# Two feed-forward layers behind a memory attention: operand sums on VectorE, one room for k and v, one weight set converted at another place

## The chip, the cores and the metric

One core of a Trainium2 chip. The metric is the device time of one execution in microseconds (us), for which three runs are given; the profile is of one further execution. The engines are TensorE (PE, with its weight loads PEld), VectorE (DVE), ScalarE (ACT), GpSimd (POOL) and SyncE (SP), which issues every transfer (DMA). Each engine works through its own list of instructions in order.

## The reference

Eight batches of eight heads, 576 positions, head size 64 and 32 memories. The result of the attention, [4608, 512], goes through two feed-forward layers, 512 to 2048 to 512.

```python
a = exp(phi - max(phi, axis=2)); a = a / (sum(a, axis=2) + 1e-9)
k_m = einsum('bhsm,bhsd->bhmd', a, k)
v_m = einsum('bhsm,bhsd->bhmd', a, v)
scores = scale * (q @ k_m.T)
x = softmax(scores) @ v_m                 # then [4608, 512]
for w_in, w_out in ((moe_w_in, moe_w_out), (moe2_w_in, moe2_w_out)):
    h = x @ w_in                          # 512 x 2048, float64
    g = h * sigmoid(1.702 * h)            # second layer: sigmoid(h)
    x = g @ w_out                         # 2048 x 512, float64
```

## The kernel before

A product of float32 matrices is taken in three passes (`PASSES`): each operand is split into a high half in the type fp32r and a low half, the rest; high x high, high x low and low x high are added in PSUM. The high half is a copy on ACT, the low half a subtraction (`sub`, line 64), so nearly all subtractions of the kernel are recorded at L64 and the additions at L61. Three of the four big products use a scheme of seven products of half size in place of eight, in the order `ORDER` = 1, 2, 6, 5, 7, 3, 4; it needs sums of quarters of both operands. The weights come as 64-bit numbers; `wconv0` and `wconv1` turn them into float32 by two ACT operations, two of VectorE (L101, L102) and an addition on POOL (L104).

The program has four stages, told apart by PE's line.

Stage 1 (L332, 42 to 421 us): attention, and the first product of layer 1. It has 256 slots, 32 for each batch, of six matmuls; from slot 24 on the order on every engine is the order in which the code is written. `at(slot, when, fn)` plans a function at a slot; `emit` calls, in each slot, those of "e", then the slot's matmuls, then those of "p", "l" and "d". `plan_attention(b)` sets the steps of batch b against z = 32b - 32: load of phi, of k and v (`load_kv`), maximum over the positions (`fold_step`), exponential, the matmuls of k and v (`kv_mm`, L207), softmax, and so on. k and v come in four parts of four heads and three chunks each, with two rooms. The gated result g (L337, L338) goes from four rooms to memory (L342). The second weight matrix of layer 1 comes in four sets of four raw loads (`wo_load`, L76); sets 0 to 2 are converted during stage 1 and their sums and lows made, set 3 around the end of the stage.

Stage 2 (L514, 421 to 849): second product of layer 1. Its 168 steps are six blocks of seven products times four parts p; `seq` lists them. A step's operand is made two steps ahead by `make`: `a_prep` takes a room, ACT copies the high half (L498, tile `op`), VectorE subtracts the low half (L64). The quarters of the gated result, a11, a12, a21, a22, are loaded as `r` or `rr` (`r_fetch`). Their sums are made in place: a21 + a22 and a21 - a11 in `a_prep` behind products 1 and 2, and a22 - a11 and a12 - a11 in `a_sum` ahead of products 7 and 3:

```python
        if then:
            a_sum(*then, early)
        sub(nc.vector, t[:, :, 1], s, rd(t[:, :, 0]))
        if b >= early and i == 1:
            add(nc.gpsimd, a21, a21, a22)
        if b >= early and i == 2:
            sub(nc.gpsimd, a11, a21, a11)
```

After the four parts of a product `evac2` adds the bank to the output tile (L529). During the stage 16 raw weights of layer 2 are converted, one every seven steps. In the last block the first two weight sets of layer 2 (`w_sums`, `w_high`, `w_low`) and the operand x of stage 3 (`x_comb`, `x_high`, `x_low`) are made.

Stage 3 (L602, 849 to 1229): first product of layer 2, 48 groups of seven products. Stage 4 (L674, 1233 to 1594): second product of layer 2, with operands made three steps ahead by the same `make`.

## Time and profile before

| | |
|---|---|
| three runs | 1601.50, 1603.86, 1605.55 us (median 1603.86) |
| the profiled execution | 1600.37 us, its span 1598.6 us |
| PE busy | 1454.8 us, 91% of the span |
| DVE, ACT, POOL busy | 1214.5, 797.3, 633.0 us |
| transfers | 264.50 MB, 165 GB/s on the mean |

Busy time is the sum over an engine's instructions; that of PE also counts matmuls at a lower clock, which take longer. A group of instructions (line, engine, operation, tiles out<-in) has its count, busy time, the mean of one in ns, the idle time of the engine just before its members and what ended that. The windows give, for a stretch, the busy time of each engine with the count of its instructions, the granted share of PE's clock, the busy share of the DMA engines, and GB/s. Several instructions with one row in a timeline have their total.

### The profile page before, as it was taken

To read this page: it belongs to the slowest core of one execution; us is meant where nothing else is said; L and a number is where in the kernel's file an instruction comes from. 1 tells how busy PE (TensorE), PEld (TensorE's weight loads), DVE (VectorE), ACT (ScalarE), POOL (GpSimd) and SP (SyncE) were. 2 spreads that over 40 slices of the span, in tenths; PEclk is the share of its full clock that TensorE was granted. 3 is DMA by queue.
4 is the path that set the end of the run, shared out by engine and by line. 5 is a ranking of instruction groups with operands and counts; after the bars stand their busy time and mean duration, and the time that the engine had idled before them with its cause. 6 is when DMAs were issued, how large, how long until landed. Compare 5 with 4: busy or idle time off the path is not lost. (4 is left out here: it accounts for less than half of the span.)

```text
span 1598.6 us, 27727 instructions
## 1 busy us (share of the span) xinstructions
PE 1454.8 (91%) x10432; PEld 1354.1 (85%) x10432; DVE 1214.5 (76%) x1529; ACT 797.3 (50%) x1415; POOL 633.0 (40%) x360
## 2 busy tenths in 40 slices
PE   4788888899799999999889899999997999999998
PEld 2566777778688899888788899999997999999998
DVE  6766666577578887988897777778688877887875
ACT  4545556566534444454445556555565444444443
POOL 2423536342475454754752333333232141242250
PEclk7799999899799999999999999999998999999999
DMA  8686687764806356264433454655456245145240
GB/s 242 178 226 211 197 228 234 208 192 152 296 21 223 113 194 204 91 229 127 140 102 115 144 180 165 203 174 172 170 180 233 95 153 188 65 144 188 67 142 30
DMA packets 214470, 264.50 MB, mean 165 GB/s; under 512 B 51520, under 2 KB 185664, under 8 KB 214336
## 3 DMA queue, kind: packets, MB, share of 16 engines
q1 hardware_dynamic: 214336, 262.73, 50.8%
q8 instruction: 82, 1.34, 0.4%
q14 instruction: 52, 0.43, 0.1%
HBM read 159.91 MB, written 102.76 MB: 164 GB/s over the span
## 5 line engine op out<-in xcount | busy, mean ns | idle before, releaser
L514 PE MATMUL p<-op,wq 128*128 128x384 f32 x2016 | 381.4, 347 | 47.0 <-DVE op L64 39.9
L514 PEld LDWEIGHTS p<-op,wq 128*128 128x128 f32 x2016 | 359.9, 194 | 68.4 <-DVE op L64 58.2
L674 PE MATMUL p<-wq,op 128*128 128x256 f32 x3024 | 360.6, 282 | 4.8 <-DVE gq L616 4.8
L674 PEld LDWEIGHTS p<-wq,op 128*128 128x128 f32 x3024 | 360.4, 191 | 5.1 <-DVE gq L616 5.1
L64 DVE TENSOR_TENSOR op<-rr,op 128x768 fp32r<-128x768 f32 x216 | 298.1, 1398 | 66.8 <-ACT op L498 64.4
L498 ACT CAST op<-rr 128x768 fp32r<-128x768 f32 x216 | 178.3, 834 | 195.0 <-PE p L674 81.8
L332 PE MATMUL h<-attnT,slab 128*128 128x288 f32 x1536 | 247.3, 313 | 10.5 <-DVE g L338 9.5
L332 PEld LDWEIGHTS h<-attnT,slab 128*128 128x128 f32 x1536 | 219.0, 198 | 40.8 <-DVE g L338 21.0
L602 PE MATMUL xb<-xq,wq 128*128 128x384 f32 x1152 | 221.5, 340 | 18.3 <-POOL xq L64 7.1
L64 DVE TENSOR_TENSOR op<-r,op 128x768 fp32r<-128x768 f32 x120 | 176.0, 1478 | 73.4 <-ACT op L498 72.4
L602 PEld LDWEIGHTS xb<-xq,wq 128*128 128x128 f32 x1152 | 201.4, 189 | 26.9 <-ACT e L634 9.5
L338 DVE SCALAR_TENSOR_TENSOR g<-g,h 128x288 f32<-128x288 f32 x256 | 110.8, 445 | 103.4 <-ACT g L337 101.5
L602 PE MATMUL y<-xq,wq 128*128 128x384 f32 x864 | 166.5, 337 | 0.9 <-ACT e L662 0.7
L616 DVE SCALAR_TENSOR_TENSOR gq<-gq,e 128x384 f32<-128x384 f32 x144 | 135.9, 957 | 36.9 <-ACT gq L611 34.3
L337 ACT ACTIVATE g<-h 128x288 f32<-128x288 f32 x256 | 103.2, 414 | 113.3 <-PE h L332 76.8
L498 ACT CAST op<-r 128x768 fp32r<-128x768 f32 x120 | 99.5, 833 | 118.4 <-PE p L674 49.1
L602 PEld LDWEIGHTS y<-xq,wq 128*128 128x128 f32 x864 | 151.7, 188 | 1.7 <-ACT e L662 1.0
L64 POOL TENSOR_TENSOR wq<-wst,wq 128x512 fp32r<-128x512 f32 x59 | 86.0, 1463 | 129.7 <-ACT wq L426 109.9
L61 POOL TENSOR_TENSOR rr<-rr,r 128x768 f32<-128x768 f32 x22 | 52.9, 2430 | 213.3 <-DMA r<-gs 172.9
L611 ACT ACTIVATE gq<-e 128x384 f32<-128x384 f32 x144 | 75.2, 525 | 115.1 <-DVE e L61 112.2
L104 POOL TENSOR_TENSOR wst<-wst 128x512 int32<-128x512 int32 x24 | 34.1, 1423 | 195.0 <-DVE wst L102 113.3
L426 ACT CAST wq<-wst 128x512 fp32r<-128x512 f32 x83 | 51.2, 618 | 47.5 <-DVE wst L64 28.1
(119 smaller groups left out, 1584.1 us busy)
## 6 DMA issues: line engine op xcount, KB each, us to landing
rr<-gs SPq DMA_DIRECT2D x120, 384.0 KB, 6.2
gs<-g SPq DMA_DIRECT2D x128, 288.0 KB, 4.0
gs<-gq SPq DMA_DIRECT2D x192, 192.0 KB, 2.0
r<-gs SPq DMA_DIRECT2D x72, 384.0 KB, 5.4
xs<-o SPq DMA_DIRECT2D x24, 384.0 KB, 4.2
xr<-xs SPq DMA_DIRECT2D x24, 384.0 KB, 4.6
out_dram<-o SPq DMA_DIRECT2D x24, 384.0 KB, 3.6
q<-in_q_dram SPq DMA_DIRECT2D x124, 72.0 KB, 4.2
```

The costliest lines, as they stand in the source:

```text
L61: eng.tensor_tensor(out=out, in0=a, in1=b, op=ALU.add)
L64: eng.tensor_tensor(out=out, in0=a, in1=b, op=ALU.subtract)
L332: nc.tensor.matmul(out=h, lhsT=slab[b, f // 4, g][:, wi, f0:f0 + 128], rhs=x[:, g, xi], start=(g == 0 and n == 0), stop=(g == 1 and n == 2))
L337: nc.scalar.activation(out=t, in_=h, func=ACTF.Tanh, scale=0.851)
L338: nc.vector.scalar_tensor_tensor(out=t, in0=t, scalar=1.0, in1=h, op0=ALU.add, op1=ALU.mult)
L426: nc.scalar.copy(out=t[:, :, 0], in_=wst[m, c, k])
L498: nc.scalar.copy(out=t[:, :, 0], in_=s)
L514: nc.tensor.matmul(out=out[:, d, :HB], lhsT=w[:, s, wi, d * 128:(d + 1) * 128], rhs=t[:, s, gi], start=(start and p == 0 and s == 0 and n ...
L602: nc.tensor.matmul(out=out, lhsT=w[:, s, wi, f0:f0 + 128], rhs=x[:, s, xi], start=(start and s == 0 and n == 0), stop=(s == 1 and n == 2), ...
L611: nc.scalar.activation(out=t, in_=h, func=ACTF.Tanh)
L616: nc.vector.scalar_tensor_tensor(out=t, in0=t, scalar=1.0, in1=h, op0=ALU.add, op1=ALU.mult)
L674: nc.tensor.matmul(out=out[:, d], lhsT=t[:, u, gi, d * 128:(d + 1) * 128], rhs=w[:, u, wi], start=(start and d != 1 and p == 0 and u == 0 ...
```

## The change

All operand sums and low halves that POOL made in stages 2 to 4 go to VectorE; POOL keeps the addition of the weight conversion (L104), the lows of weight sets 0 to 2 in stage 1, and parts of the softmax. k and v get one room for four heads and all six chunks; of batches 0 and 1 the second four heads go to rooms that the weights take later. The maximum over the positions is taken in five operations of one chunk in place of three of different sizes, and the steps of the attention stand some slots earlier. g gets a fifth room. Set 3 of the weights is converted early in the last batch, into rooms of `attnT`, and moved by two transfers from SBUF to SBUF (`wo_move`) into the tile where it is used. The first eight operands of stage 2 stand in another order. The line numbers of the changed kernel differ by up to ten: L332 there is the store of g, L328 its gating on VectorE, L127 the load of k and v, L532 the addition out of PSUM.

```diff
-    def load_kv(b, g, c0):
-        t = att.tile([P, 2, 4, 3, D], F32, tag="kv", name="kv", bufs=2)
+    def load_kv(b, g):
+        t = att.tile([P, 2, 4, C6, D], F32, tag="kv", name="kv")
         for i, src in enumerate((k, v)):
...
+    def load_kv_early(b, rooms):
+        t = st["kv", b, 1] = [wo_p.tile([P, 2, C6, D], F32, tag=f"wo{n}", name="kve") for n in rooms]
...
+    def fold(b, name, op, eng):
+        x = st["phi", b]
+        t = st[name, b] = att.tile([P, H, M], F32, tag=name, name=name)
+        for c in range(1, C6):
+            eng.tensor_tensor(out=t, in0=t if c > 1 else x[:, :, 0], in1=x[:, :, c], op=op)
...
-            gt[b, f] = moe.tile([128, 2, HS], F32, tag="g", name="g", bufs=4)
+            gt[b, f] = moe.tile([128, 2, HS], F32, tag="g", name="g", bufs=5)
...
     def wo_conv0(c, k):
-        if k == 0:
+        if c == 3 and k % 2 == 0:
+            st["wos", c, k // 2] = moe.tile([128, 2, 2, 256], F32, tag="attnT", name="wos", bufs=4)
+        elif c < 3 and k == 0:
...
+    def wo_move():
+        t = stage()
+        for i in range(2):
+            nc.sync.dma_start(out=t[:, 2 * i:2 * i + 2], in_=st.pop(("wos", 3, i)))
+        wst[2, 3] = [t[:, n] for n in range(5)]
...
-    def a_sum(b, i, p, m):
+    def a_sum(b, i, p):
         if i == 7:
-            sub(nc.vector if m else nc.gpsimd, ra[b, 2, p], ra[b, 3, p], ra[b, 0, p])
+            sub(nc.vector, ra[b, 2, p], ra[b, 3, p], ra[b, 0, p])
...
-        if b >= early and i == 1:
-            add(nc.gpsimd, a21, a21, a22)
-        if b >= early and i == 2:
-            sub(nc.gpsimd, a11, a21, a11)
+        if b and i == 1:
+            add(nc.vector, a21, a21, a22)
+        if b and i == 2:
+            sub(nc.vector, a11, a21, a11)
 
     seq = [(b, i, p) for b in range(NBK) for i in ORDER for p in range(4)]
+    seq[:8] = [(0, i, p) for i in (1, 2) for p in range(3)] + [(0, 1, 3), (0, 2, 3)]
...
-        fold, mt, mr, mb, sb, ex, mm, es, norm, kt, ke = (
-            ((-4, -3, -3), -1, 0, 1, (2, 3), (3, 4), (4, 5, 6, 7), 5, 8, 10, 11) if first else
-            ((-21, -20, -20), -18, -16, -13, (-11, -9), (-9, -7), (-7, -6, -2, -1), -6, 0, 3, 4))
-        load(-24 if b == 2 else -27, load_phi, b)
+        pm, mt, mr, mb, sb, ex, mm, es, norm, kt, ke = (
+            (-4, -1, 0, 1, (2, 3), (3, 4), (4, 7), 5, 8, 10, 11) if first else
+            (-17, -14, -12, -10, (-9, -8), (-8, -7), (-6, 1), -7, 2, 4, 5) if b == 2 else
+            (-27, -24, -22, -19, (-17, -15), (-15, -13), (-11, -2), -12, 0, 3, 4))
+        load({2: -24, 3: -31}.get(b, -34), load_phi, b)
...
+        load({2: -28, 3: -31}.get(b, -34), load_kv, b, 0)
+        if first:
+            load(-34, load_kv_early, b, (11, 12, 13, 14))
+        else:
+            load(mm[0], load_kv, b, 1)
...
-    w_set(2, 148, (170, 173, z + 21, z + 22, z + 23, z + 24, z + 25),
...
+    w_convert(3, (z - 1, z - 1, z + 4, z + 6), (z + 3, z + 5, z + 8, z + 10))
+    for n in range(2, 6):
+        w_step(2, n, z + 18 + n, nc.vector, 1, 2)
...
-        at(z + 20 + n, "d", r_fetch, 0, 0, qq, p)
-    for n in range(4):
-        at(z + (18, 18, 27, 28)[n], "d", wo_load, 3, n)
-        at(z + (27, 28, 30, 31)[n], "e", wo_conv0, 3, n)
-        at(z + (27, 28, 30, 31)[n], "l", wo_conv1, 3, n)
+        at(z + 19 + n, "d", r_fetch, 0, 0, qq, p)
+    at(z + 29, "d", wo_move)
...
-    at(z + 28, "e", make, 0, ROOMS[0], 0)
-    at(z + 30, "e", make, 0, ROOMS[0], 1)
+    at(z + 26, "e", make, 0, ROOMS[0], 0)
+    at(z + 29, "e", make, 0, ROOMS[0], 1)
...
-    for n, x in enumerate((0, 1, 5, 9, 13, 17, 20)):
-        at(x, "e", w_make, 2, 3, n, nc.gpsimd, nc.vector)
+    for n, x in enumerate((3, 4, 8, 11, 14, 17, 20)):
+        at(x, "e", w_make, 2, 3, n, nc.vector, nc.vector)
...
-            at(LAST + s + 3 + n, "l", w_low, 0, c, n, nc.gpsimd)
+            at(LAST + s + 3 + n, "l", w_low, 0, c, n, nc.vector)
...
-        at(LAST + x, "l", x_low, 0, i, nc.gpsimd if i in (6, 7, 4) else nc.vector)
+        at(LAST + x, "l", x_low, 0, i, nc.vector)
...
-            at1(n + 3 + j, 3, x_comb, b, j, nc.gpsimd)
+            at1(n + 3 + j, 3, x_comb, b, j, nc.vector)
```

VectorE at the boundary of two blocks of stage 2 (`op` are low halves, `r` and `rr` loaded quarters), before:

```order
L64 TENSOR_TENSOR op_5783<-r_5629,op_5783 128x2x384
L64 TENSOR_TENSOR op_5799<-r_5647,op_5799 128x2x384
L64 TENSOR_TENSOR op_5818<-rr_5692,op_5818 128x2x384
L64 TENSOR_TENSOR op_5837<-rr_5692,op_5837 128x2x384
L64 TENSOR_TENSOR op_5853<-rr_5649,op_5853 128x2x384
L64 TENSOR_TENSOR op_5869<-rr_5649,op_5869 128x2x384
L64 TENSOR_TENSOR op_5890<-rr_5695,op_5890 128x2x384
L101 TENSOR_SCALAR stg_5887<-stg_5887 128x512
```

and in the changed kernel:

```order
L64 TENSOR_TENSOR op_5765<-r_5611,op_5765 128x2x384
L61 TENSOR_TENSOR r_5530<-r_5530,rr_5710 128x768
L64 TENSOR_TENSOR op_5781<-r_5629,op_5781 128x2x384
L61 TENSOR_TENSOR r_5551<-r_5551,rr_5710 128x768
L64 TENSOR_TENSOR op_5800<-rr_5674,op_5800 128x2x384
L61 TENSOR_TENSOR r_5572<-r_5572,rr_5747 128x768
L64 TENSOR_TENSOR op_5819<-rr_5674,op_5819 128x2x384
L61 TENSOR_TENSOR r_5593<-r_5593,rr_5747 128x768
L64 TENSOR_TENSOR op_5835<-rr_5631,op_5835 128x2x384
L64 TENSOR_TENSOR r_5611<-r_5530,r_5611 128x768
L64 TENSOR_TENSOR op_5851<-rr_5631,op_5851 128x2x384
L64 TENSOR_TENSOR r_5629<-r_5551,r_5629 128x768
```

Six sums, which stood in POOL's list at the same place, stand now between the low halves; the four at L61 read a quarter of the next block that has just been loaded (`rr_5710`, `rr_5747`).

VectorE around the first steps of stage 2 (`g` is the gated result, `wst` the stage tile of weight set 3, `wq` a weight half), before:

```order
L64 TENSOR_TENSOR op_5251<-r_5113,op_5251 128x2x384
L338 SCALAR_TENSOR_TENSOR g_5262<-g_5262,h_5255 128x288
L101 TENSOR_SCALAR wst_5194<-wst_5194 128x2x256
L102 SCALAR_TENSOR_TENSOR wst_5194<-raw_5211,wst_5194 128x2x256
L338 SCALAR_TENSOR_TENSOR g_5262<-g_5262,h_5273 128x288
L101 TENSOR_SCALAR wst_5194<-wst_5194 128x2x256
L102 SCALAR_TENSOR_TENSOR wst_5194<-raw_5235,wst_5194 128x2x256
L64 TENSOR_TENSOR wst_5194<-wst_5194 128x512 x2
L64 TENSOR_TENSOR op_5305<-rr_5126,op_5305 128x2x384
```

and in the changed kernel:

```order
L64 TENSOR_TENSOR op_5280<-rr_5121,op_5280 128x2x384
L64 TENSOR_TENSOR op_5296<-rr_5138,op_5296 128x2x384
L64 TENSOR_TENSOR op_5311<-rr_5138,op_5311 128x2x384
L61 TENSOR_TENSOR r_5172<-r_5172,rr_5184 128x768
L64 TENSOR_TENSOR wst_5242<-wst_5242 128x512 x2
L64 TENSOR_TENSOR wq_5329<-wst_5242,wq_5329 128x2x256
L64 TENSOR_TENSOR op_5332<-rr_5153,op_5332 128x2x384
```

The conversion of set 3 (L101, L102) has left this place, low halves stand next to each other, and the sums of the set stand behind the third of them.

SP in the second batch of stage 1, around the loads of k and v of a later batch and of w_out (`raw`), before:

```order
L128 DMA kv_1646<-in_k_dram 96x4x192
L128 DMA kv_1646<-in_v_dram 96x4x192
L76 DMA raw_1649<-in_moe_w_out_dram 128x1024
L342 DMA gs0_5_90<-g_1588 128x576
L128 DMA kv_1695<-in_k_dram 96x4x192
L128 DMA kv_1695<-in_v_dram 96x4x192
```

and in the changed kernel, with all four heads in one load for k and one for v:

```order
L76 DMA raw_1567<-in_moe_w_out_dram 128x1024
L76 DMA raw_1569<-in_moe_w_out_dram 128x1024
L127 DMA kv_1606<-in_k_dram 96x4x384
L127 DMA kv_1606<-in_v_dram 96x4x384
L332 DMA gs0_4_89<-g_1532 128x576
L332 DMA gs0_5_90<-g_1564 128x576
L76 DMA raw_1663<-in_moe_w_out_dram 128x1024
```

Before, the third raw load stood between the two halves of k and v; now k and v stand ahead of it.

## Rows read from the trace of the kernel before

**Rows 1.** The page, section 1: busy us and share of the span by engine.
```profile
PE 1454.8 (91%) x10432; PEld 1354.1 (85%) x10432; DVE 1214.5 (76%) x1529; ACT 797.3 (50%) x1415; POOL 633.0 (40%) x360
```

**Rows 2.** Windows: stages 2, 1, 4; length, busy by engine, clock, DMA share, GB/s.
```profile
421.10:849.30 428.20, 381.20 (x2018) 359.80 (x2017) 355.78 (x277) 190.82 (x258) 247.00 (x117) 0.96 0.44 148
42.40:421.10 378.70, 330.70 (x3203) 272.29 (x3202) 254.86 (x538) 211.08 (x488) 143.13 (x115) 0.93 0.70 207
...
1233.50:1594.10 360.60, 360.57 (x3024) 360.36 (x3024) 276.89 (x245) 153.69 (x189) 103.34 (x42) 0.99 0.36 124
```

**Rows 3.** Windows: a stretch of stage 3 in which PE never waits; columns as above.
```profile
1000.00:1040.00 40.00, 40.00 (x231) 40.00 (x230) 30.96 (x43) 23.05 (x47) 14.44 (x9) 1.00 0.61 205
```

**Rows 4.** Windows of L514 alone: blocks 0, 4 and 5; length, PE, PEld, clock, DMA, GB/s.
```profile
421.10:505.40 84.30, 68.72 (x337) 63.96 (x338) 0.87 0.46 157
...
703.50:768.90 65.40, 61.46 (x338) 58.00 (x337) 1.00 0.49 170
768.90:849.30 80.40, 65.72 (x337) 62.08 (x335) 0.94 0.26 80
```

**Rows 5.** Waits of PE, 421 to 850: us, times, longest.
```profile
PE p L514 <- DVE op L64: 39.9, 45, 5.1
```

**Rows 6.** Groups of DVE by shape, 1248 to 1290: busy, mean ns, idle before.
```profile
L64 DVE TENSOR_TENSOR op<-rr,op 128x768 fp32r<-128x768 f32 x15 | 14.1, 953 | 2.7 <-ACT op L498 2.7
```

**Rows 7.** The same of DVE, 1290.8 to 1310.
```profile
L64 DVE TENSOR_TENSOR op<-rr,op 128x768 fp32r<-128x768 f32 x6 | 13.2, 2234 | 2.0 <-ACT op L498 1.9
```

**Rows 8.** The same of POOL, 1290.8 to 1310.
```profile
L61 POOL TENSOR_TENSOR rr<-rr,r 128x768 f32<-128x768 f32 x4 | 9.6, 2428 | 43.5 <-DMA r<-gs 43.5
```

**Rows 9.** The same of DVE, then of POOL, 421 to 850 (stage 2).
```profile
L64 DVE TENSOR_TENSOR op<-rr,op 128x768 fp32r<-128x768 f32 x96 | 142.6, 1510 | 25.2 <-ACT op L498 23.3 <-DMA rr<-gs 1.1
...
L104 POOL TENSOR_TENSOR stg<-stg,wst 128x512 int32<-128x512 int32 x8 | 15.2, 1904 | 29.7 <-issue 29.7
```

**Rows 10.** Waits of PE, 42 to 421 (stage 1).
```profile
PE a L207 <- DMA kv<-in_v_dram: 12.8, 5, 5.9
PE h L332 <- DVE g L338: 9.5, 8, 3.0
PE aa L257 <- DVE slab L64: 8.7, 6, 3.4
```

**Rows 11.** Timeline of PE at 160: start, us, engine, line, tiles, [idle before].
```profile
160.88 1.51 PE L207 MATMUL a<-kv,phi 96*32 96x128 f32 x24 [5.87 <-DMA kv<-in_v_dram]
```

**Rows 12.** Timeline of SP at 153.
```profile
153.22 0.35 SPq L76 DMA_DIRECT2D raw<-in_moe_w_out_dram  x1
...
154.10 0.42 SPq L128 DMA_DIRECT2D kv<-in_k_dram  x1
```

**Rows 13.** Windows: the us after that wait; columns as in rows 2.
```profile
160.90:165.00 4.10, 4.10 (x36) 3.70 (x37) 1.20 (x4) 0.00 (x0) 0.81 (x1) 0.50 0.72 161
```

**Rows 14.** Timeline of DVE in stage 4.
```profile
1249.87 0.95 DVE L64 TENSOR_TENSOR r<-rr,r 128x768 f32<-128x768 f32 x1
1250.74 0.95 DVE L64 TENSOR_TENSOR op<-r,op 128x768 fp32r<-128x768 f32 x1
```

**Rows 15.** Timeline of DVE early in stage 2: conversion and one weight sum.
```profile
434.34 0.42 DVE L101 TENSOR_SCALAR wst<-wst 128x512 int32<-128x512 int32 x1
434.79 0.69 DVE L102 SCALAR_TENSOR_TENSOR wst<-raw,wst 128x512 int32<-128x512 int32 x1
435.40 0.69 DVE L64 TENSOR_TENSOR wst<-wst 128x512 f32<-128x512 f32 x1
```

**Rows 16.** Timeline of PE, then of ACT, at the start of stage 2.
```profile
430.46 0.69 PE L514 MATMUL p<-op,wq 128*128 128x384 f32 x1 [3.70 <-ACT op L498]
...
428.47 0.66 ACT L93 ACTIVATE wst<-raw 128x512 f32<-128x512 f32 x1 [6.98 <-DMA raw<-in_moe_w_out_dram]
```

**Rows 17.** Windows of L332 alone: the last 32 slots of stage 1.
```profile
388.10:421.10 33.00, 27.13 (x194) 26.09 (x192) 0.98 0.71 255
```

**Rows 18.** Waits of PE, 850 to 1240 (stage 3).
```profile
PE xb L602 <- POOL xq L64: 7.1, 5, 1.7
```

More of the change, by code (lines that the diff above doesn't have):

```diff
@@ L202, in kv_mm @@
         e = st["phi", b]
-        kv = st.pop(("kv", b, g, c0))
-        for c in range(c0, c0 + 3):
+        kv = st.pop(("kv", b, g))
+        for c in range(C6):
             for j in range(4):
-                rhs = kv[j // 2][:, :, j % 2, c - c0, :] if isinstance(kv, list) else kv[:, :, j, c - c0, :]
                 nc.tensor.matmul(out=a[32 * j:32 * j + 32, 256 * g:256 * g + 2 * D], lhsT=e[:, 4 * g + j, c, :],
-                                 rhs=rhs, start=(c == 0), stop=(c == C6 - 1))
+                                 rhs=kv[j][:, :, c, :], start=(c == 0), stop=(c == C6 - 1))
     def es_mm(b):
@@ L490, in attn_moe_moe, with a_prep @@
     nop = [0]
-    def a_prep(b, i, p, then, rooms, early):
+    def a_prep(b, i, p, then, rooms):
         a11, a12, a21, a22 = (ra.get((b, x, p)) for x in range(4))
@@ L732, in load @@
             at(max(z + s, -6), "d", fn, *a)
[L734 to L739 removed]
+        pm, mt, mr, mb, sb, ex, mm, es, norm, kt, ke = (
[3 more added lines that the diff above has]
+        load({2: -24, 3: -31}.get(b, -34), load_phi, b)
+        at(z + pm, "e", fold, b, "pm", ALU.max, nc.vector)
         at(z + mt, "p", phi_max_t, b)
@@ L745, in plan_attention @@
             at(z + ex[g], "e", phi_exp, b, g)
-        for n in range(3):
-            at(z + es, "e", fold_step, b, "es", ALU.add, nc.gpsimd, n)
-        for n, (g, c) in enumerate(((0, 0), (0, 3), (1, 0), (1, 3))):
-            load((-24, -24)[n] if b == 2 and n < 2 else (-34, -33)[n] if n < 2 else mm[n - 2], load_kv, b, g, c)
-            at(z + mm[n], "p", kv_mm, b, g, c)
-        at(z + mm[3], "p", es_mm, b)
+        at(z + es, "e", fold, b, "es", ALU.add, nc.gpsimd)
+        load({2: -28, 3: -31}.get(b, -34), load_kv, b, 0)
[3 more added lines that the diff above has]
+            load(mm[0], load_kv, b, 1)
+        for g in range(2):
+            at(z + mm[g], "p", kv_mm, b, g)
+        at(z + mm[1], "p", es_mm, b)
         at(z + norm, "e", kv_norm, b)
@@ L813, in attn_moe_moe @@
     at(z + 4, "e", phi_fold0, "es", ALU.add)
-    for n, (g, c) in enumerate(((0, 0), (0, 3), (1, 0), (1, 3))):
-        at(z + 4, "p", kv_mm, 0, g, c)
+    for g in range(2):
+        at(z + 4, "p", kv_mm, 0, g)
     at(z + 5, "p", es_mm, 0)
```

91 lines of the change are left out of this document (39 added, 52 removed).

## The prediction

> **What bounds the kernel now.** I read four views in this order: the page's busy shares, the windows by stage, the waits of TensorE (PE), and the groups of VectorE (DVE) and GpSimd (POOL) in one stage. PE is busy for 91% of the span [rows 1], so what can be won is its idle time, and the time in which its clock is low after an idle stretch. The windows say where that lies [rows 2]: stage 4 has 360.57 busy us in 360.60 and stands at its floor, stage 2 has 381.2 in 428.2, stage 1 330.7 in 378.7.
>
> *Stage 2* runs in six blocks of 28 steps, a step being 12 matmuls of 384 columns. In a stretch where PE never waits 231 such matmuls take 40.0 us [rows 3], 0.1732 each, so a step is 2.08 and a block 58.2. The blocks take 84.3, four times about 65.9 ((428.2 - 84.3 - 80.4) / 4) and 80.4 [rows 2, 4]. What PE waits for is the low half of its operand from VectorE, 39.9 us in 45 waits [rows 5]; the rest of the excess is the clock, .87 in the first block and .94 in the last [rows 4]. So VectorE is late, though its share is 76%. Why: the same operation (128x768, both inputs in SBUF) takes 953 ns in a stretch in which POOL stands idle [rows 6], and 2234 ns right after it [rows 7], where POOL, after 43.5 idle us, runs its own sums at 2428 ns each [rows 8]. In stage 2 it takes 1510 ns on the mean of 96 [rows 9], because POOL makes the operand sums there.
>
> *Stage 1* loses 12.8 us waiting for k and v, 9.5 for g and 8.7 for the slab [rows 10]. The longest wait for k and v, 5.87 us [rows 11], has a cause on SP: the load of w_out went out at 153.22 and held up the second half of k and v, issued at 154.10 [rows 12]. Then PE runs at .50 of its clock, 1.2 of 2.4 GHz, having idled [rows 13].
>
> **The change, part by part.**
>
> *Sums to VectorE in the middle blocks of stage 2.* Per block VectorE had 28 low halves and 4 sums, and gets 12 more (three kinds for four row groups): 44 operations. Back to back they start 0.87 us apart when POOL is quiet [rows 14], so 38.3 us. To it come 4 additions out of PSUM at the same 0.87 (3.5), and 4 weight conversions of 0.42 + 0.69 [rows 15], 4.4. POOL keeps only the conversions' additions, 4 a block of 1904 ns [rows 9]. A low half under a POOL operation loses 2234 - 953 = 1.3 us, so 5.2. Sum 51.4 of 58.2: VectorE has slack again, and PE should stand near its floor. I allow 1.2 us of ragged steps: 59.4 against 65.9, **-6.5 for each of four blocks, -26**. For the price of a POOL operation, the Trainium skill (SBUF — State Buffer, section on the two separate sides) says that the shared port is a lock: who comes second is blocked for the whole instruction. By that the four cost 4 x 1.9 = 7.6 and the sum is 53.8, still below the floor.
>
> *Last block of stage 2.* It carries two weight sets of layer 2 and the sums of the next x, whose lows go to VectorE as well: 28 lows 24.4, 16 sums 13.9, 4 PSUM additions 3.5, 22 weight operations at 0.61 (one takes 0.69 [rows 15], less the 0.08 by which 953 exceeds 870) 13.4, x sums 4 x 0.87 and x lows 6 x 0.87. That is 63.9, over the floor; with some idle time around it I take 67 against 80.4, **-13**. Bounds: 60 and 76.
>
> *First block.* At present set 3 of the weights is converted in the last slots of stage 1 and the first steps of stage 2. ACT waits 6.98 us for its raw load, the operand's copy queues behind the conversion, and PE waits 3.70 [rows 16]. The change converts it some 24 slots earlier and only moves it, by two 512 KB transfers, into the stage tile. These now stand behind eleven loads of 384 KB which begin at slot z+19, about 408. That is 5.3 MB; at the 255 GB/s of the last stage-1 window [rows 17] it is 20.6 us, so the move lands at 429 to 431. VectorE's queue has the two sums of set 3 ahead of the operand of step 5, which PE wants at 421.1 + 5 x 2.08 = 431.5. Two sums, a weight low, the operand's low and the waits between them put it at 435 to 438. So I expect a new stall of 4 to 7 us there (I take 7, and 2 for the low clock after it) and 2.4 at the next operand behind a weight low: 58.2 + 9 + 2.4 + 2 of ragged steps = 72 against 84.3, **-12**. Bounds: 60 (no stall) and 84 (as now).
>
> *Stage 1.* With one room for four heads and steps planned earlier, the load of the second four heads of k and v goes out ahead of the blocked raw load. The two long waits go, and with them about 3 us of half clock each (4.1 us at .50 alone is 2.05 [rows 13]): 12.8 + 6, less 1 that stays, is -18. Of the 9.5 for g and 8.7 for the slab I take two thirds, -12. They belong to moments when maxima, conversions and softmax stand ahead on VectorE; the fifth gated room and the early conversion (the last slots have no conversion of set 3 left) thin them out, while the fold on VectorE grows from three operations to five. **-30**, between -12 (the two long waits alone) and -42 (all three kinds, and the clock).
>
> The second half of k and v now goes out only after the first half's matmuls, since there is one room. Two loads of half the size took from 154.10 to 160.88, 6.8 us [rows 11, 12], to arrive. Twice the bytes at 255 GB/s [rows 17] add 2.3, so 9.1. PE wants them 9 slots later, and a slot is at least 33.0 / 32 = 1.03 us [rows 17], so 9.3. That is just enough.
>
> *Stage 3.* PE waits 7.1 us for x lows on POOL, 5 times [rows 18]; they go to VectorE, which has them done in 0.87. With the clock after them **-9**; bounds -4 and -10.
>
> *Stage 4* has no stall in its blocks; the moved sums fit in VectorE's idle time (276.9 busy of 360.6 [rows 2]). **0**, at worst +4 at its start, where the first sums of the block wait for a load.
>
> **Sum**: -30 - 12 - 26 - 13 - 9 = -90 from the profiled execution's own 1600.4, which is 1510. The three runs have their median 3.5 above it; I put half of that on: **1512**.
>
> **Rivals.**
>
> *A, more comes out.* All stalls of stage 1 go and the start of stage 2 doesn't stall: stage 1 -42, block 0 -24, block 5 -16, the rest as above, -117, with the same step to the median: **1485**. For it: VectorE's slack. Against: the move behind 4.3 MB of loads.
>
> *B, VectorE stands in waits for loads.* The sums of a21 + a22 wait for r loads, and they are now in VectorE's queue ahead of lows for which PE waits; on POOL such a wait hurt nobody. With 3 us and 1 of clock for each of 5 block boundaries, 20 us, and the start of stage 2 and the last block as now (+12, +3), -55: **1547**. Against it: operands are prepared two steps ahead, 4.2 us, of which copy and low take 1.8.
>
> *C, one room for k and v.* If double the bytes take double the time, 13.6 us instead of 9.1, each of six batches waits 4 us and has 2 of low clock. That is 36 us, stage 1 gives +6 instead of -30: **1548**. For it: the wait would come in each batch, where now it comes in two. Against: the transfers overlap.
>
> *D, the slower side: VectorE is slow by itself in stage 2.* If the 1.5 us come from what it does there and not from POOL, 44 operations of 1.5 us, with 3.5 and 4.4, are 74 a block against 65.9: +8 four times. Block 0 then keeps -4, the last block has 54 such operations, 81 + 13.4 + 3.5 = 98: +18; stage 3 -5, stage 1 -30. Sum +11: **1613**. It decides as soon as these operations take over (58.2 - 7.9) / 44 = 1.14 us each, and turns the sign at about 1.45. For it: VectorE takes on 12 operations a block and is already the engine that PE waits for. The Trainium skill (Perfetto Trace Analysis) has such a rule: if VectorE is saturated, giving work to GpSimd may make sense, though the port they share may undo it. Against: the same operation, in two stretches of stage 4 that follow each other, changes from 953 to 2234 ns [rows 6, 7], with POOL's sums as the one thing that comes.
>
> *E, the change does only half of what it says.* The conversions' additions stay on POOL and hold VectorE up more than 1.3 us each, so the four middle blocks win 3 and not 6.5, the last one 8, stage 3 nothing; with stage 1 and the first block as above -62: **1540**.
>
> **How the numbers follow.** Forecast .60, A .10, B .14, C .09, D .04, E .03. The range goes from 1480, which is A with the middle blocks at 58.2 (4 x 1.2 less), to 1552, which takes in B, C and E with a few us to spare (the first block at its upper bound and stage 1 at -12 are 1542); it leaves out D. This kernel's runs tell a difference of about 0.3% (5 us) from none. Faster by more than that: all but D and the worst of B and C together, .94; within it .02, slower .04.
>
> **What would show it.** In the changed profile the 128x768 lows in stage 2 should take about 1.0 us on the mean; a middle block 59 to 60 us with PE clock 1.0; the last block 67, and VectorE close to fully busy in it; one stall near step 5 of stage 2, where VectorE waits for the moved set. In stage 1 the waits for k and v should be under 3 us in all, and those for x on POOL in stage 3 gone. I am wrong if lows stay over 1.2 us (D), if VectorE's largest idle in stage 2 is for r loads (B), or if PE waits for k and v once in each batch (C).

## The result and the profile after

The changed kernel takes 1552.4 us (median of four runs, 1551.3 to 1554.8), against 1602.7 before (1600.8 to 1605.6): a ratio of 0.9687 with an interval of 0.9666 to 0.9707. That is about 50 us faster, where 90 were forecast; the time lies at the upper edge of the range, just outside it (1552). The profiled execution has a span of 1553.0 us, at the upper end of its runs.

The page's first section and the windows by stage answer to [rows 1, 2]; columns are the same.

```profile
PE 1446.3 (93%) x10432; PEld 1355.6 (87%) x10432; DVE 1158.2 (75%) x1742; ACT 797.8 (51%) x1415; POOL 206.3 (13%) x175
```

```profile
424.75:812.10 387.35, 365.54 (x2018) 352.43 (x2017) 314.10 (x365) 186.97 (x251) 27.72 (x16) 0.99 0.48 165
42.60:424.75 382.15, 338.05 (x3203) 278.77 (x3202) 262.55 (x563) 214.49 (x493) 147.64 (x130) 0.91 0.70 207
1187.50:1548.40 360.90, 360.28 (x3023) 360.08 (x3024) 260.85 (x288) 153.58 (x189) 0.00 (x0) 0.99 0.36 124
```

In the order of the rows, stage 2 went from 428.2 to 387.4 us, stage 1 from 378.7 to 382.2, stage 4 stayed at 360.9. What lies between, stage 3 with the passage to stage 4, went from 384.2 (849.3 to 1233.5) to 375.4 (812.1 to 1187.5). So the gain is all in stages 2 and 3, and stage 1, from which a third of it was expected, gave none. VectorE does more instructions in stage 2 (365, before 277) in less busy time (314 us, before 356).

The windows of stage 2's matmuls by block answer to [rows 4] (blocks 0, 4 and 5).

```profile
424.75:496.90 72.15, 62.67 (x337) 59.85 (x338) 0.95 0.54 189
679.50:740.20 60.70, 59.52 (x338) 58.26 (x336) 1.00 0.53 183
740.20:812.20 72.00, 64.43 (x337) 59.32 (x336) 0.98 0.29 90
```

The groups of VectorE by shape in stage 2 answer to [rows 9]; the waits of TensorE there answer to [rows 5].

```profile
L64 DVE TENSOR_TENSOR op<-rr,op 128x768 fp32r<-128x768 f32 x96 | 95.5, 1000 | 29.8 <-ACT op L500 29.3
...
L64 DVE TENSOR_TENSOR rr<-r,rr 128x768 f32<-128x768 f32 x12 | 15.9, 1322 | 0.0
```

```profile
PE p L517 <- DVE op L64: 12.8, 26, 1.4
PE p L517 <- ACT op L500: 8.7, 7, 3.9
```

A low half takes 1000 ns where it took 1510, though VectorE has more to do, and PE waits 12.8 us for it, before 39.9. The one group that is still slow, twelve sums at 1322 ns, is a place where POOL's remaining additions fall: four of the twelve, each under one of these additions, take 2.06 or 2.07 us, and the other eight 0.95.

In stage 1 the waits of TensorE answer to [rows 10]. The wait for k and v (L207 before, L197 now) is not in the list any more; in its place stand VectorE's transpose (L264; at L274 before, with 4.5 us) and ACT's tanh (L327):

```profile
PE aa L247 <- DVE nat L264: 14.8, 7, 4.2
PE h L322 <- DVE g L328: 10.4, 9, 2.5
PE a L236 <- ACT g L327: 4.4, 2, 2.2
```

PE's idle time in stage 1, the length less its busy time in the windows (above, and [rows 2]), fell from 48.0 to 44.1 us. Its busy time rose from 330.7 to 338.1 us, at a granted clock of 0.91 in place of 0.93. So some waits were exchanged for others, and a lower clock took what was left.

### The profile page after: what moved, and what is told of

The parts are those of the page before. It is cut to its first block, busy times and chain, and to the rows that moved or that the text cites. A ratio compares the mean times of both kernels' runs of the same rounds, so it can differ in the third digit from the quotient of the medians.

```text
span 1553.0 us, 27494 instructions
## 1 busy us (share of the span) xinstructions
PE 1446.3 (93%) x10432; PEld 1355.6 (87%) x10432; DVE 1158.2 (75%) x1742; ACT 797.8 (51%) x1415; POOL 206.3 (13%) x175
## 5 line engine op out<-in xcount | busy, mean ns | idle before, releaser
L517 PE MATMUL p<-op,wq 128*128 128x384 f32 x2016 | 365.8, 340 | 21.8 <-DVE op L64 12.8
L517 PEld LDWEIGHTS p<-op,wq 128*128 128x128 f32 x2016 | 352.5, 189 | 34.9 <-DVE op L64 23.4
L64 DVE TENSOR_TENSOR op<-rr,op 128x768 fp32r<-128x768 f32 x216 | 209.9, 975 | 82.0 <-ACT op L500 79.4
L322 PEld LDWEIGHTS h<-attnT,slab 128*128 128x128 f32 x1536 | 225.2, 203 | 50.9 <-DVE g L328 25.3
L322 PE MATMUL h<-attnT,slab 128*128 128x288 f32 x1536 | 254.2, 318 | 11.6 <-DVE g L328 10.4
L328 DVE SCALAR_TENSOR_TENSOR g<-g,h 128x288 f32<-128x288 f32 x256 | 110.2, 444 | 98.9 <-ACT g L327 98.1
L64 DVE TENSOR_TENSOR op<-r,op 128x768 fp32r<-128x768 f32 x120 | 116.7, 975 | 61.1 <-ACT op L500 60.9
L327 ACT ACTIVATE g<-h 128x288 f32<-128x288 f32 x256 | 103.0, 415 | 106.4 <-PE h L322 66.7
L619 DVE SCALAR_TENSOR_TENSOR gq<-gq,e 128x384 f32<-128x384 f32 x144 | 93.8, 657 | 27.3 <-ACT gq L614 24.6
L104 POOL TENSOR_TENSOR wst<-wst 128x512 int32<-128x512 int32 x24 | 34.1, 1420 | 503.1 <-DVE wst L102 242.7
L61 DVE TENSOR_TENSOR e<-e,y 128x384 f32<-128x384 f32 x96 | 52.3, 550 | 17.9 <-PE y L605 15.0
L247 PE MATMUL aa<-w,kvT 64*32 64x512 f32 x512 | 41.1, 673 | 19.7 <-DVE nat L264 15.8
```

What stands on the lines that cost most here:

```text
L61: eng.tensor_tensor(out=out, in0=a, in1=b, op=ALU.add)
L64: eng.tensor_tensor(out=out, in0=a, in1=b, op=ALU.subtract)
L322: nc.tensor.matmul(out=h, lhsT=slab[b, f // 4, g][:, wi, f0:f0 + 128], rhs=x[:, g, xi], start=(g == 0 and n == 0), stop=(g == 1 and n == 2))
L327: nc.scalar.activation(out=t, in_=h, func=ACTF.Tanh, scale=0.851)
L328: nc.vector.scalar_tensor_tensor(out=t, in0=t, scalar=1.0, in1=h, op0=ALU.add, op1=ALU.mult)
L517: nc.tensor.matmul(out=out[:, d, :HB], lhsT=w[:, s, wi, d * 128:(d + 1) * 128], rhs=t[:, s, gi], start=(start and p == 0 and s == 0 and n ...
```

## Where stage 1's gain went

One of the longest of the new waits, 3.93 us, can be followed through four engines. First SP's timeline:

```profile
162.99 0.35 SPq L121 DMA_DIRECT2D phi<-in_phi_dram  x1
163.39 0.53 SPq L127 DMA_DIRECT2D kv<-in_k_dram  x1
163.97 1.15 SPq L127 DMA_DIRECT2D kv<-in_v_dram  x1
165.16 1.86 SPq L332 DMA_DIRECT2D gs<-g  x1
```

phi, k and v of a later batch, three times 576 KB, go out one behind the other, and a store of the gated result g stands behind them. The view of the DMA issues from 160 to 178 us (KB each, median us from issue to landing) shows what that means:

```profile
gs<-g SPq DMA_DIRECT2D x6, 288.0 KB, 7.8
...
phi<-in_phi_dram SPq DMA_DIRECT2D x1, 576.0 KB, 8.6
kv<-in_k_dram SPq DMA_DIRECT2D x1, 576.0 KB, 10.6
kv<-in_v_dram SPq DMA_DIRECT2D x1, 576.0 KB, 11.5
```

Stores of g, which land after 4.0 us in the median of the whole execution, need 7.8 here, and the one issued at 165.16 needs 11.1. Their room is then not free when ACT wants to write the next g into it. The timelines of ACT, VectorE and PE follow:

```profile
176.37 0.71 ACT L327 ACTIVATE g<-h 128x288 f32<-128x288 f32 x2 [5.37 <-DMA gs<-g]
```

```profile
176.81 0.45 DVE L328 SCALAR_TENSOR_TENSOR g<-g,h 128x288 f32<-128x288 f32 x1 [2.62 <-ACT g L327]
...
178.25 0.84 DVE L264 STREAM_TRANSPOSE nat<-aa 128x288 f32<-128x288 f32 x2
```

```profile
179.23 1.96 PE L247 MATMUL aa<-w,kvT 64*32 64x512 f32 x16 [3.93 <-DVE nat L264]
```

ACT stands 5.37 us for the store. VectorE, which works in order, waits for that tanh ahead of the transpose that empties a PSUM tile, and PE waits 3.93 us for the tile. ACT's waits for stores of g in stage 1, before the change and after it:

```profile
ACT g L337 <- DMA gs<-g: 34.4, 16, 5.2
...
ACT g L327 <- DMA gs<-g: 36.9, 16, 6.0
```

So these waits are not new. Before the change, with four rooms, ACT waited as often and nearly as long. What is new is that four of them, of 4.6 to 6.0 us, end just ahead of a transpose for which PE then waits 2.1 to 4.2 us. That is only a reading of traces; the experiments below move its parts one by one.

## The experiments

Ratios are to the kernel before, run on the same chip in the same session; the interval stands behind each. The changed kernel has 0.9687, from a session of its own; it was not timed again beside the experiments. "Stage 1" is the time from its first to its last matmul of the first product, 378.7 before and 382.1 in the changed kernel's profile; other profiles that share this stage up to its last slots (move_ahead, sums_undone) have 378.4 and 375.8, so differences of up to 6 us there mean nothing.

**sums_alone.** The kernel before, with only the engine of the sums changed:

```diff
-            sub(nc.vector if m else nc.gpsimd, ra[b, 2, p], ra[b, 3, p], ra[b, 0, p])
+            sub(nc.vector, ra[b, 2, p], ra[b, 3, p], ra[b, 0, p])
...
-            add(nc.gpsimd, a21, a21, a22)
+            add(nc.vector, a21, a21, a22)
...
-            sub(nc.gpsimd, a11, a21, a11)
+            sub(nc.vector, a11, a21, a11)
```

and in the same way the lows and sums of the last block of stage 2 and of stage 3.

> The kernel before, with nothing changed but the engine of the sums and low halves of stages 2 to 4 (VectorE instead of GpSimd); k and v, the gated rooms and weight set 3 stay as before. Theory 1 (the whole gain of the change comes from the sums; the rest of it wins in stage 1 nothing): stage 1 stays at 378.7 us, the middle blocks of stage 2 go to 60 to 61, the last to about 72, stage 3 loses its waits for x; the first block gains little, since set 3 is still converted there: 36 to 40 us less than before, about 1564, which is 0.976. Rival (the sums bring only part and the other parts the rest): 25 us or less, above 1577.

Measured: 1557.5 us, 0.9692 (0.9669 to 0.9716). The windows of its blocks 0, 4 and 5 of stage 2:

```profile
424.27:502.90 78.63, 67.50 (x337) 64.02 (x338) 0.84 0.50 169
685.30:746.00 60.70, 59.52 (x337) 58.25 (x337) 1.00 0.54 184
746.00:816.50 70.50, 62.87 (x338) 57.76 (x336) 1.00 0.30 92
```

The sums alone give the ratio of the whole change. It is a little more than expected, since block 0 wins too (84.3 to 78.6).

**sums_undone.** The other way round, the changed kernel with the same lines turned back (`nc.vector` to `nc.gpsimd`), except that the sums of the first block of stages 2 and 4 stay on VectorE.

> The changed kernel with the sums and low halves of stages 2 to 4 back on GpSimd as before; k and v, the rooms and set 3 as changed. Theory 1 (the sums alone made the gain): the middle blocks of stage 2 take about 66 us again, the last 78 to 80, stage 3 its 7 us; 40 to 48 us slower than the changed kernel, ratio 0.993 to 1.0. Rival (the parts help each other: with set 3 early the blocks no longer need it): 30 us slower or less, below 0.988.

Measured: 1597.2 us, 0.9943 (0.9926 to 0.9961). Its second block of stage 2 takes 65.5 us, its last 82.1. So the sums are worth 0.0256 of the time of before on the changed kernel, some 41 us, and 0.0308 on the kernel before, some 49. All the rest of the change brings 0.6% without them and nothing that can be told with them. Shown both ways: the sums made the gain. That the rest brings nothing is a balance of gains and losses, as the next runs show.

**kv_undone.** The changed kernel with k and v, the maximum and the plan of the attention as before:

```diff
-        t = att.tile([P, 2, 4, C6, D], F32, tag="kv", name="kv")
+        t = att.tile([P, 2, 4, 3, D], F32, tag="kv", name="kv", bufs=2)
...
-            (-27, -24, -22, -19, (-17, -15), (-15, -13), (-11, -2), -12, 0, 3, 4))
+            ((-21, -20, -20), -18, -16, -13, (-11, -9), (-9, -7), (-7, -6, -2, -1), -6, 0, 3, 4))
```

> The changed kernel with k and v, their rooms, the maximum and the steps of the attention as before; five gated rooms, early set 3 and the sums as changed. Theory 1 (in stage 1 the change trades the two long waits for k and v for waits for the gated rooms): the waits for k and v come back (12 us), those of VectorE's transpose in front of the slab products (14.8 us) go to about 4, and the total stays within 6 us of the changed kernel, 1546 to 1558. Rival (the new rooms of k and v did win the 18 us that were forecast, and something else in stage 1 lost them again): 10 us or more slower than the changed kernel, over 1563.

Measured: 1549.3 us, 0.9647 (0.9628 to 0.9666). Its waits of TensorE in stage 1:

```profile
PE a L207 <- DMA kv<-in_v_dram: 15.3, 6, 6.0
PE h L332 <- DVE g L338: 8.2, 10, 2.5
PE aa L257 <- DVE slab L64: 6.5, 7, 2.8
PE aa L257 <- POOL w L104: 4.7, 1, 4.7
PE a L246 <- ACT qT L250: 2.7, 1, 2.7
PE aa L257 <- DVE nat L274: 1.8, 5, 1.0
```

The waits for k and v are back with 15.3 us, the one for the transpose went from 14.8 to 1.8, and the time is the same or a trifle shorter. The change has traded one wait for another. ACT waits for stores of g only 7.5 us in this stage 1, where the kernel before, with four rooms and the same plan of the attention, has 34.4. The sums and set 3 differ as well, but they stand in other stages or in the last slots. So with the old plan the fifth room seems to have thinned these waits out, and the new plan of k and v brought them back to 36.9. The slots ahead of the last 32 take 335.7 us here, 345.7 before and 338.8 to 344.1 in the profiles of the changed plan.

**kv_load_later.** One number: when the first four heads of k and v are loaded (the third batch keeps its own).

```diff
-        load({2: -28, 3: -31}.get(b, -34), load_kv, b, 0)
+        load({2: -28, 3: -24}.get(b, -24), load_kv, b, 0)
```

> The changed kernel with one number changed: the load of the first four heads of k and v goes out at z-24 in place of z-34 (z-31 for the third batch), so ten slots behind that of phi. Theory 1 (phi, k and v together, 1.7 MB in one burst, stand ahead of the stores of g; ACT's tanh waits for a gated room, VectorE and TensorE behind it): ACT's waits of 5.4 and 6.0 us for stores of g go below 3, the waits of TensorE for the transpose of VectorE fall from 14.8 to under 6, stage 1 is 8 to 15 us shorter, 1538 to 1545. Rival (VectorE is late by its own list, five operations of the maximum and the conversions ahead of the transpose): no difference over 3 us.

Measured: 1531.9 us, 0.9541 (0.9521 to 0.9561), 23 us less than the changed kernel by the ratios. Stage 1 takes 360.7 us. The waits of ACT for stores and of PE for the transpose, in stage 1:

```profile
ACT g L327 <- DMA gs<-g: 10.1, 8, 2.3
```

```profile
PE aa L247 <- DVE nat L264: 4.8, 7, 1.2
```

Both are as theory 1 said, and the gain is larger than expected. VectorE's own list, with the five operations of the maximum, was not touched, so the rival falls. The window of this stage 1, with the columns of [rows 2]:

```profile
43.50:404.25 360.75, 327.36 (x3204) 270.59 (x3203) 263.94 (x563) 214.07 (x492) 147.56 (x130) 0.97 0.74 220
```

Half of the 21.4 us by which it is shorter than in the changed kernel's profile is idle time of PE (33.4 us, there 44.1). The other half is its busy time (327.4, there 338.1), at a granted clock of 0.97 in place of 0.91. The gain is larger than the waits alone.

**kv_three_slots_later.** The same number at z-31 for the batches that had z-34.

```diff
-        load({2: -28, 3: -31}.get(b, -34), load_kv, b, 0)
+        load({2: -28, 3: -31}.get(b, -31), load_kv, b, 0)
```

> The changed kernel with the load of the first four heads of k and v at z-31 in place of z-34, three slots behind phi in place of the same slot (third batch as it is). Theory 1 (the transfers of phi, k and v, 1.7 MB, stand as one burst ahead of the stores): three slots are about 4 us, the burst needs 6 to 8, so most of it stays: 1542 to 1550. Rival (not the transfers, but SP: at z-34 the load waits for its room, which the last matmuls of the batch before are just leaving, and the stores queue behind that wait on SP): at z-31 the room is free, so nearly the whole gain of kv_load_later comes, below 1538.

Measured: 1539.1 us, 0.9599 (0.9568 to 0.9630), between the two expectations: faster than theory 1 allowed, and not quite the rival's. The lines tell why neither was right:

```profile
ACT g L327 <- DMA gs<-g: 35.1, 15, 5.1
```

```profile
PE aa L247 <- DVE nat L264: 4.7, 6, 1.2
```

ACT still waits 35.1 us for stores, nearly as long as in the changed kernel, so the burst is still there, as theory 1 has it. But PE's wait for the transpose is as small as with z-24. What differs is the place at which ACT's wait falls. In the changed kernel ACT's wait ended at 176.37, and the transposes and PE's product came behind it (178.25, 179.23). Three slots on, PE has that product before the wait of ACT ends:

```profile
173.27 1.09 PE L247 MATMUL aa<-w,kvT 64*32 64x512 f32 x16 [1.21 <-DVE nat L264]
...
174.80 0.41 ACT L327 ACTIVATE g<-h 128x288 f32<-128x288 f32 x1 [5.04 <-DMA gs<-g]
```

PE's idle time in stage 1 is 39.3 us, before this edit 44.1; the rest of the gain is its busy time, 322.8 us at a granted clock of 0.96. SP's wait for the room of k and v (PE, L197) did not get smaller: 9.9 us from 100 to 340 us in the changed kernel, 11.5 here, so the rival's reason isn't seen.

**four_rooms.** The changed kernel without the fifth gated room.

```diff
-            gt[b, f] = moe.tile([128, 2, HS], F32, tag="g", name="g", bufs=5)
+            gt[b, f] = moe.tile([128, 2, HS], F32, tag="g", name="g", bufs=4)
```

> The changed kernel with four gated rooms, as before the change, in place of five. Theory 1 (ACT's tanh waits for a gated room while the stores of g stand in the burst of phi, k and v; so the count of rooms decides how much of the burst reaches TensorE): a room fewer, which is two slots or about 2 us less of cover in each of five bursts, makes stage 1 longer by 6 to 14 us: 1558 to 1567. Rival (the rooms do nothing; the waits come from VectorE's list or ACT's): within 3 us of the changed kernel, 1549 to 1556.

Measured: 1589.7 us, 0.9893 (0.9872 to 0.9913): 33 us slower than the changed kernel, more than twice the most that theory 1 gave. Stage 1 takes 418.4 us. ACT's waits for stores are 72.4 us in place of 36.9. The direction was right; the size says that theory 1 is not the whole account.

**later_four_rooms.** Four rooms, with k and v at z-24 (both edits above).

> kv_load_later with four gated rooms in place of five. Theory 1 (the fifth room only covers the burst, which made four rooms 37 us slower in the changed kernel): with the burst taken apart a room less costs under 12 us, ratio below 0.962. Rival (four rooms are too few for the new steps of the attention wherever the loads stand): 25 us or more, above 0.970.

Measured: 1561.3 us, 0.9733 (0.9707 to 0.9760). Without the burst the missing room still costs 0.0192, 31 us, against kv_load_later. Theory 1 fails here. SP's timeline and its waits at the raw loads (L76) in this run point to another reason:

```profile
146.53 1.01 SPq L332 DMA_DIRECT2D gs<-g  x2
158.17 0.33 SPq L76 DMA_DIRECT2D raw<-in_moe_w_out_dram  x1
158.55 0.42 SPq L332 DMA_DIRECT2D gs<-g  x1
```

```profile
SPq L76 <- POOL wst L104: 37.7, 6, 10.1
```

Between two stores of g SP issues nothing for more than ten microseconds: it stands at the third raw load of a weight set, whose room POOL frees only with the conversion's addition (L104). The stores behind it are ready and can't go out: VectorE gated four halves of g from 149.20 on. The addition was late in its turn. ACT had waited for a store until 154.74, VectorE's gating for ACT until 155.19, and VectorE's part of the conversion (156.01) and POOL's addition (156.84) came behind it. So late stores and SP's stand feed each other here. The stand itself is older than the change; SP's waits at L76 in stage 1, before and after:

```profile
SPq L76 <- POOL wst L104: 27.1, 6, 7.2
...
SPq L76 <- POOL wst L104: 21.8, 4, 8.1
```

**raw_later_four_rooms.** Theory 2: that stand is what the gated rooms have to cover. The third and fourth raw load are planned when their rooms are free:

```diff
-        w_convert(c, (x, x, x + 5, x + 9), (x + 6, x + 10, x + 14, x + 18))
+        w_convert(c, (x, x, x + 8, x + 12), (x + 6, x + 10, x + 14, x + 18))
```

> later_four_rooms with the third and fourth raw load of w_out of each set planned at x+8 and x+12 in place of x+5 and x+9, when their rooms should be free. Theory 2 (in stage 1 SP stands up to 10 us at a raw load whose room POOL still holds; the stores of g queue up behind it, and the gated rooms have to cover that): SP's 37.7 us of waiting at L76 fall under 8, stage 1 goes from 389.6 to 375 or less, ratio under 0.965. Rival (four rooms are short for the transfers themselves, or for the steps of the attention): the wait on SP goes and the time stays, ratio 0.970 or more.

Measured: 1544.9 us, 0.9614 (0.9590 to 0.9639), 19 us less. Stage 1 takes 373.5 us. SP's wait at these loads:

```profile
SPq L76 <- POOL wst L104: 3.7, 2, 2.8
```

The wait on SP and the time fell as theory 2 said; with four rooms and both loads moved, this kernel now beats the changed one with five. But ACT still waits 27.7 us for stores in its stage 1, and the kernel with five rooms, both loads moved and the move of set 3 ahead (below) has 0.9480. Of that difference of 0.0134 the move has 0.002 to 0.003, so about 17 us of the fifth room's worth remain, by an estimate from these ratios. Neither of the two theories explains them.

**raw_later.** The same edit on the changed kernel, with five rooms and k and v at z-34.

> The changed kernel (five rooms, k and v at z-34) with the same later raw loads. Theory 1 (the burst of phi, k and v alone makes the loss): within 4 us of the changed kernel; it may be slower, as the fourth raw load now stands behind the burst. Theory 2 (SP's stand at the raw load has its part): 5 to 12 us faster, about 1540 to 1547.

Measured: 1541.8 us, 0.9599 (0.9582 to 0.9616), 14 us less than the changed kernel, a little above theory 2's range in gain. ACT's waits for stores go from 36.9 to 18.9 us in stage 1, though the burst is untouched. So the stores were late for two reasons, the burst in the transfers and SP's stand. How the time came from the second with five rooms is not shown, for ACT now waits for the raw loads, and PE's wait for the transpose did not fall:

```profile
ACT wst L93 <- DMA raw<-in_moe_w_out_dram: 13.2, 2, 7.1
...
PE aa L247 <- DVE nat L264: 18.9, 8, 5.9
```

Stage 1 takes 373.0 us, against 375.8 to 382.1 in the three profiles of the changed plan; PE's idle time (43.2 us) is that of the changed kernel, and its busy time is lower (329.7).

**set3_later.** The changed kernel with the third and fourth conversion of set 3 five slots later.

```diff
-    w_convert(3, (z - 1, z - 1, z + 4, z + 6), (z + 3, z + 5, z + 8, z + 10))
+    w_convert(3, (z - 1, z - 1, z + 4, z + 6), (z + 3, z + 5, z + 13, z + 15))
```

> The changed kernel with the third and fourth conversion of weight set 3 at slots z+13 and z+15 in place of z+8 and z+10. Theory 1 (ACT stands 5.1 us for the raw load at z+8, whose load had to wait for the room of the first ones; tanh stands behind it): the last 32 slots of stage 1 go from 38.0 to about 33.5 us, the total down by 4 to 5, about 1548. Rival (the loads of r, which begin at z+19, then hold up the stores of g, or the conversion hinders wherever it is): less than 2 us.

Measured: 1548.1 us, 0.9637 (0.9615 to 0.9659). The windows of the last 32 slots of stage 1 and of block 0 of stage 2:

```profile
380.24:413.00 32.76, 31.09 (x243) 26.37 (x242) 23.80 (x49) 21.94 (x51) 11.43 (x8) 1.00 0.80 259
413.00:488.10 75.10, 65.73 (x338) 62.34 (x338) 54.03 (x67) 30.59 (x43) 1.98 (x1) 0.93 0.54 189
```

The last slots come down from 38.0 to 32.8 us as expected (before: 33.0 [rows 17]); the early conversion had cost 5 us there, because ACT stood 5.06 us for the raw load. Block 0 gives 3 of them back, 75.1 for 72.1. The ratio fell by 0.0050, 8 us, which is more than these two windows account for; where the rest came from was not tried.

**move_ahead.** The move of set 3 ahead of the last four loads of r.

```diff
-        at(z + 19 + n, "d", r_fetch, 0, 0, qq, p)
-    at(z + 29, "d", wo_move)
+        at(z + 19 + n if n < 7 else z + 21 + n, "d", r_fetch, 0, 0, qq, p)
+    at(z + 27, "d", wo_move)
```

> The changed kernel with the move of set 3 planned at z+27, ahead of the last four loads of r (a21 and a22), in place of z+29 behind them. Theory 1 (the first block stalls because the move stands behind the eleven loads; it was issued at 430.0 and landed at 439.0, 14.3 us after the stage began): it lands about 4 us earlier and the first block takes 67 to 69 us in place of 72.1, about 1548. Rival (the sums of a21 and a22 then wait for their loads, which are now later, and the stall only moves): within 1.5 us.

Measured: 1549.6 us, 0.9640 (0.9619 to 0.9661). Block 0 takes 67.7 us in place of 72.1, as expected. The stall at steps 4 and 5 was the move standing behind loads; the whole gains 8 us by the ratios, twice what the block does.

**kv_and_set3_later, all_three, later_move_ahead, later_ahead_raw_later.** Combinations of the edits above.

> Both changes of number together: k and v at z-24, conversions of set 3 at z+13 and z+15. If the two losses are separate, their gains add: kv_load_later's ratio of 0.954 less the 0.003 of set3_later, 0.951, about 1526 us; stage 1 at 355 us. If they overlap, as kv_load_later alone: 0.954.

> k and v at z-24, set 3 at z+13 and z+15, the move at z+27. If the losses add up: 0.951 less 0.002 to 0.003 for the earlier move, 0.948, about 1522 us. A rival for the last part: with the later conversion the moved set is only just ready, and the move waits for POOL's addition instead of the loads; then as kv_and_set3_later.

> k and v at z-24 and the move of set 3 at z+27, conversions as in the changed kernel. If the losses are separate: kv_load_later's 0.954 less the 4 us that move_ahead took from the first block, 0.951 to 0.952, about 1527. The time would then equal all_three, which also has the conversions later: that part would add nothing. Rival: 0.954, the gain of the first block goes elsewhere.

> later_move_ahead with the later raw loads: k and v at z-24, move at z+27, raw at x+8 and x+12. By theory 2 another 2 to 6 us off its 0.9517, so 0.948 to 0.950, as five rooms cover most of SP's stand already; by the rival no difference.

Measured, in this order: 0.9536 (0.9516 to 0.9557), 0.9509 (0.9485 to 0.9532), 0.9517 (0.9495 to 0.9540), 0.9480 (0.9454 to 0.9506). The later conversion adds nothing to the later load of k and v (0.9536 against 0.9541): its profile has the last 32 slots at 32.7 us in place of 39.1, but the batches before them take nearly 3 us more and block 0 of stage 2 and the last block 1.5 each. Why the last 1.5 come was not tried. The move ahead adds its 4 us (0.9517; block 0 takes 67.2 us in place of 72.1), with the later conversion too (0.9509). The later raw loads bring a few more, as theory 2 said of five rooms, though the intervals of 0.9517 and 0.9480 overlap a little. With the load of k and v they add about 6 us, by themselves 14, so the two gains seem not to add in full. The last of the four has a median of 1524.0 us against 1606.0 before in its session; it has the lowest median of this study, with k and v at z-24, the raw loads at x+8 and x+12 and the move at z+27, three edits of numbers on the changed kernel. Its stage 1 takes 355.9 us, ACT waits 5.6 us for stores of g, and block 0 takes 67.0.

## Why the prediction was wrong

**Middle blocks of stage 2: right in the cause, a little too good in the size.** Predicted 59.4 us a block, measured 60.7 to 61.1, and a clock of 1.00; the four together won 20 us, not 26. VectorE was slow because of POOL, as rows 6 and 7 had it: lows at 1000 ns, where 1.0 us was said. The price of a POOL operation was set too high: the excess over 950 ns of all 128x768 operations of stage 2 with two inputs in SBUF, chiefly 96 x 50, 70 x 33, 24 x 49 and 12 x 372 ns, is 12.8 us for 16 additions, 0.8 each, where the forecast had 1.3. That is a mean of unlike cases: under nine of the additions one operation of VectorE takes 2.06 to 2.08 us in place of 0.95, under four about 1.5, and under three none is longer. By the rule of the Trainium skill (SBUF — State Buffer, section on the two separate sides) it would be up to the 1.9 of a whole instruction; that agrees with the trace as a bound, 1.13 us being the most that one operation lost, and not as a mean. What remains over the floor are two pairs of steps in each block, 1.1 us and 1.2 us, where the forecast had ragged steps of 1.2 in all. In each of the four blocks these pairs follow the two additions that cost a whole 1.1 us (in block 2 the additions stand at 572.22 and 600.95, and PE waits at 575.78 and 603.65). The step that failed is "VectorE has slack again": the sum left 6.8 us of it, and these two losses still reached PE.

**Block 0: right, in part by luck.** 72 was forecast, with a stall at step 5 where VectorE waits for the moved set; measured 72.15, and the timeline of VectorE has the stall:

```profile
430.85 0.95 DVE L61 TENSOR_TENSOR r<-r,rr 128x768 f32<-128x768 f32 x1
437.86 0.69 DVE L64 TENSOR_TENSOR wst<-wst 128x512 f32<-128x512 f32 x1 [6.06 <-DMA wst<-wos]
```

The move went out at 430.02 and VectorE got its first half at 437.86, 13.1 us after the stage began, later than the 8 to 10 us of the forecast. PE's stall there, 3.92 and 1.40 us, is still within the 4 to 7 that were allowed. move_ahead showed that its place among the loads decides.

**Last block: too good.** 67 was forecast and 72.0 measured. VectorE is busy for 61.7 of the 72.0 us, near the 63.9 of the sum, but not "close to fully busy": in 9.5 us, eight times, it waits for ACT's copies of operands. Three of these copies (4.3 us) had waited on PE, for a room or a bank. The other five (5.2 us) stood in ACT's list behind an operation that had waited for VectorE itself, four times a weight half behind its sum and once the output. The two engines waited for each other in turn, so an engine needed for 64 us did not fill 67. The step that failed is "with some idle time around it I take 67".

**Stage 3: right** (-9 forecast, about -9 measured with the passage to stage 4): PE's wait for x lows on POOL, 7.1 us, is gone, and 3.7 us for those on VectorE stand in its place, before 0.9. Stage 4 stayed, as forecast.

**Stage 1: wrong, and this is the failure of the sum.** -30 was forecast, +3.5 measured in the profile, between -3 and +3.5 over the profiles that share it. The step was: "the load of the second four heads of k and v goes out ahead of the blocked raw load. The two long waits go". They did go, all 12.8 us of them. But the forecast priced the larger and earlier loads by the time k and v themselves take (9.1 us against 9.3), and put what stands behind them at nothing. The stores of g share SP's list and the DMA engines with them; their rooms are the ones that ACT writes into, and ACT's wait reaches PE by way of VectorE: the wait for the transpose went from 4.5 to 14.8 us. Moving the load (kv_load_later) took that wait down to 4.8 and gave 23 us.

The next step, "Of the 9.5 for g and 8.7 for the slab I take two thirds", came true for the slab (2.0 us now), not for g (10.4). And of what was to bring it, "the early conversion (the last slots have no conversion of set 3 left)" is wrong: the conversion still stands in the last 32 slots, only earlier in them, and they went from 33.0 to 38.0 us because ACT stood 5.06 us for its raw load (set3_later: 32.8). The fifth room seems to have had its effect with the old plan of k and v (kv_undone), and the new plan used it up.

The waits of ACT for stores, 34.4 us, and of SP at the raw loads, 27.1 us, were there before the change, and the forecast's rows have neither. Planning the raw loads later (raw_later) gave 14 us; both together with the move give 355.9 us for stage 1, -23 against before, which is near the forecast for a plan that it did not describe. The fifth room, which the forecast took as one that thins out waits for g, carries 33 us in this plan: without it the change would be 1% faster than before and not 3%.

**The rivals.** D (VectorE slow by itself) is excluded by 1000 ns. B (VectorE stands for r loads) did not come: VectorE waits 4.3 us in all for r in stage 2. C (PE waits for k and v in each batch) did not come either, the wait is not in the list. E had the conversions' additions hold VectorE up more than 1.3 us each; it is 0.8. The time is close to what B, C and E gave, but for a reason none of them had: waits for outgoing transfers at another place, and the early conversion.

## To carry to other kernels

A load that is made larger or issued earlier has to be priced by the transfers that are issued after it, the stores above all: ask which room they free and who writes into it next. A transfer that waits for a room on an in-order issuing engine holds up every store behind it, and spare rooms of the stored tile hide part of this until one is taken away. Planning the load for the time when its room is free lets the stores pass, but who needs that load then has to be looked at: in raw_later ACT waited 13.2 us for it. And before two engines share elementwise work, compare the same instruction with and without the other engine running.

## What the runs showed that was not expected

The place of a wait matters more than its size: with k and v three slots later ACT still waited 35 us for stores (36.9 in the changed kernel), but 14 us of the time were gone, and PE waited 4.7 us for the transpose in place of 14.8. The kernel before shows it too: 34.4 us of such waits, and 4.5 for the transpose. And one room of 2.3 KB per partition was worth 33 us in the changed kernel and 31 with the load of k and v moved away, more than either of the two causes by itself. About 17 us of it are left when both causes are taken away (an estimate, see raw_later_four_rooms), and what they come from stays open.
